# Chunk 7's routing logits from VectorE's dot products instead of TensorE's matmuls, in a three-stage kernel

## The chip, the cores and the metric

The kernel runs on one core of a Trainium2 chip. The metric is the device time of one execution in microseconds. Before the change three runs gave 766.73, 768.21 and 768.28 us; the median is 768.21. The profiled execution took 771.43 us.

## What is computed

The reference has three stages, one behind the other, all in float32:

```python
scores = q @ k^T / sqrt(64)           # 4 batches, 8 heads, 576 positions
scores = where(0 <= i-j < 128, scores - slope[h]*|i-j|, -1e9)
x = softmax(scores) @ v               # -> 2304 tokens x 512
h = x @ w_in                          # 512 -> 2048
x = (h * clip(h + 3, 0, 6) / 6) @ w_out
xn = x / (|x| + 1e-6); en = expert_emb / (|expert_emb| + 1e-6)
logits = xn @ en.T / tau              # 8 experts
e = argmax(logits); gate = softmax(logits)[e]
out = gate * (relu(x @ w1[e]) @ w2[e])   # each token by its one expert
```

## The kernel before, in words

The 2304 tokens are nine chunks of 256. Attention of the later chunks runs in the gaps of the dense layer of the earlier ones; for chunks 7 and 8 of the dense layer there is no attention left. A chunk's dense layer is eight up groups (`gemm1`, L720: 24 matmuls into `h_ps`) and eight down groups (`gemm2`, L773: 12 matmuls that add up in two banks `y_ps`); every float32 product is three passes over operands split in a high and a low part. Between an up group and its down group lie ScalarE's `u` (L730), VectorE's gate on `u` (L740), ScalarE's high part `gh` (L744) and VectorE's low part `gl` (L750). TensorE's stream alternates: up group i+2, down group i, up group i+3, down group i+1.

When a chunk's last down group is done, a `Route` object decides which expert takes each of its tokens. `rows` scales the two banks by 1/6 into `ys` and stores them to `ybuf`; `norms` sums their squares. The 8 logits of each token come in one of two ways:

- Chunks 0 to 6: `spread` loads half of the normalised expert embeddings, the same 4 x 512 numbers in every partition (`en_all`, a tile of 8 KB per partition, 1 MB in all), and `dots` lets VectorE multiply and sum, one instruction of 512 elements for each expert and half chunk (L834, and a short one that reads the sum).
- Chunks 7 and 8: `flip` transposes `ys` on TensorE and copies it back (`yT`), `logits` multiplies it with the embeddings (`lgT`), `total` adds four partial rows (`lg`).

`choose` takes the largest logit, its expert as a row of zeros and a one (`oh`) and the running count of tokens (`seen`). `ranks` (L880, L881) and `place` give each token its slot in its expert's list, which POOL scatters to `slots` in DRAM (L896). Behind chunk 7's `place`, `rank_experts(False)` sorts the experts by their counts so far (`ps_n`, L924). With that, SP reads the two largest experts' numbers, loads their weights (`st`, L1023, L1026) and the first lists (`ids`, L984), POOL gathers the rows (`xg`, L1001), and ScalarE and VectorE split the weights (`w_e`, L161, L162), all during chunk 8's dense layer. Chunk 8's tokens are routed while the first expert runs.

What sets the order: each piece of work is entered at a step by `at(step, ...)`, and the steps are played in order. One step unit is 1/1.91 of an up and a down group. TensorE carries out its instructions in exactly that order. On the other engines a scheduler orders the instructions by its own estimates. `ends(c)` is the step of chunk c's last down group; the numbers in `ROUTE` and `DOTS` are added to it.

The tiles for weights are one pool of 17 (`wp`, tag "w"); 16 hold the dense layer's split weights, and from chunk 1 on the one left takes the halves of `en_all`, one after the other. A weight tile is free when its last matmul of chunk 8 has read it.

Of the kernel before, what the change touches and what calls it, by code (L numbers as in the profile page):

```python
# [9 lines left out]
F32 = mybir.dt.float32  # L10
# [51 lines left out]
P_BUFS, V_BUFS = 2, 2  # L62
FLIPS_AHEAD = 0.01

ROUTE = (1, 1.43, 2.92, 4.5)
DOTS = ((-3.5, 4.5), (0.8, 1.0), (7.4, 0.8), 10.9, 12.28)
PLACE_C = 4.3

TOTAL = 0.95
PLACE_0 = (6.5, 10.6, 6.7, 2.08, 2.2, 1.0, 8.6)  # L70
# [27 lines left out]
def tile_kernel(  # L98
# [13 lines left out]
    nc = tc.nc  # L112
    B, H, S, D = q.shape
    NT, DM = out.shape
    DFF = w_in.shape[1] // 2
    NE = w1.shape[0]
# [3 lines left out]
    NCH = NT // CH  # L120
# [13 lines left out]
    wp = main.enter_context(tc.tile_pool(name="wp", bufs=17))  # L134
# [10 lines left out]
    def two_k(name, shape=(128, 512), dt=F32):  # L145
        return keep.tile(list(shape), dt, tag="f", bufs=5, name=name)

    def small(name, shape, dt=F32, bufs=2):
        return keep.tile(list(shape), dt, tag=name, bufs=bufs, name=name)
# [25 lines left out]
    for p in range(NP):  # L175
# [12 lines left out]
        out=whole, in_=whole, compare_op=ALU.is_ge, fill=MASKED, base=128, pattern=[[-1, 256]], channel_multiplier=1  # L188
    )
    nc.gpsimd.affine_select(  # L190
        out=whole, in_=whole, compare_op=ALU.is_ge, fill=MASKED, base=-1, pattern=[[1, 256]], channel_multiplier=-1
# [3 lines left out]
    for kinds in ((2, 2), (2, 0), (2, 1), (1, 2), (0, 2)):  # L195
        tables[kinds] = t = const.tile([128, 192], BF16, name="table%d%d" % kinds)
        for h, kind in enumerate(kinds):
            r = slice(64 * h, 64 * h + 64)
# [19 lines left out]
    half, share = fixed[:, 0:2], fixed[:, 2:3]  # L218
# [7 lines left out]
        out=earlier, in_=earlier, compare_op=ALU.is_gt, fill=0.0, base=0, pattern=[[1, 128]], channel_multiplier=-1  # L226
# [5 lines left out]
        out=fold, in_=ident.rearrange("p (g e) -> p e g", g=KD)[:, 0:NE, :], axis=AX.X, op=ALU.add  # L232
# [549 lines left out]
    class Route:  # L782
        def __init__(self, c):
            self.c = c

        def copy(self, t):
            c = self.c
# [25 lines left out]

        def norms(self):
            self.ss = small("ss", (128, 2))
            if self.c < NCH - 2:
                self.junk = two_k("junk")
            for t in range(2):
                ys = self.ys[t]
                to = self.junk if self.c < NCH - 2 else ys  # L820
                nc.scalar.activation(out=to, in_=ys, func=AF.Square, accum_out=self.ss[:, t:t + 1])
            self.rn = rn = small("rn", (128, 2))
            nc.gpsimd.tensor_tensor(out=rn, in0=self.ss, in1=half, op=ALU.pow)

        def spread(self, half):
            self.en = wp.tile([128, NE // 2, DM], F32, tag="w", name="en_all")
            src = en_rows[NE // 2 * half:NE // 2 * (half + 1), :].rearrange("(o e) d -> o (e d)", o=1)
            nc.sync.dma_start(out=self.en.rearrange("p e d -> p (e d)"), in_=src.to_broadcast([128, NE // 2 * DM]))

        def dots(self, e):  # L830
            if e == 0:
                self.lg = small("lg", (128, 2, NE))
            for t in range(2):
                V.tensor_tensor_reduce(  # L834
                    out=self.junk, in0=self.ys[t], in1=self.en[:, e % (NE // 2), :],
                    scale=1.0, scalar=0.0, op0=ALU.mult, op1=ALU.add, accum_out=self.lg[:, t, e:e + 1],
                )

# [319 lines left out]
    def at(step, fn, *args):  # L1158
        todo[step].append((fn, args))
# [8 lines left out]
    def ends(c, i=NF2 - 1):  # L1168
        return 0.0 if c == 0 else begins(2) if c == 1 else begins(c, i) + FIRST[2]
# [240 lines left out]
        at(begins(BLANK[0] + n // 3, BLANK[1]), blank, n, n + 3)  # L1410
    for c in range(NCH - 1):
        g = ends(c)
        if c < NCH - 2:
            loads, *halves, d2, d3 = DOTS
            if c == 0:
                g, r = FIRST[0], route_0
            else:
                r = Route(c)
                at(g, r.rows)
                at(g + 0.3, r.norms)  # L1420
                for x in range(2):
                    at(g + (loads[x] if c > 1 or x else 0.6), r.spread, x)
                for e in range(NE):
                    x, y = divmod(e, NE // 2)
                    at(g + halves[x][0] + halves[x][1] * y, r.dots, e)
            at(g + d2 * (c > 0), r.choose)
            at(g + d3 * (c > 0) + PLACE_C * (c == 0), r.ranks)
            at(g + d3 * (c > 0) + PLACE_C * (c == 0), r.place)
            continue
        r = Route(c)  # L1430
        at(g, r.rows)
        d = ROUTE
        assert 0 < d[0] <= d[1] <= d[2] < d[2] + TOTAL < d[3]
        at(g + d[0], r.flip, 0)
        at(g + d[1], r.flip, 1)
        at(g + d[1], r.norms)
        at(g + d[2], r.logits)
        at(g + d[2] + TOTAL, r.total)
        at(g + d[2] + TOTAL, r.choose)
        at(g + d[3], r.ranks)  # L1440
        at(g + d[3], r.place)
    g = begins(NCH - 1)

    def close_attention():
# [1 line left out]
        pools["x"] = main.enter_context(tc.tile_pool(name="x2", bufs=1, side="right"))  # L1446

    at(g - 1, close_attention)
    assert g + PLACE_0[0] > ends(NCH - 2) + ROUTE[3]
    at(g + PLACE_0[0], rank_experts, False)  # L1450
    at(g + PLACE_0[0], load_order, False, 0)
    at(g + PLACE_0[6], load_ids, 0, range(n_first))
# [9 lines left out]
    g = ends(NCH - 1)  # L1462
# [8 lines left out]
    r = Route(NCH - 1)  # L1471
# [34 lines left out]
    for j in range(1, NE):  # L1506
# [6 lines left out]
        if j == 1:  # L1513
            s = PLACE_1
            loads = [s[0] + s[1] * i for i in range(4)]
            splits = [s[2] + s[3] * i for i in range(8)]
            ids, gets, turns = LATE[0] + 0.05, [s[4] + s[5] * t for t in range(n)], [s[8] + s[9] * t for t in range(n)]
        else:
            s = [x + b - 16 for x in NEXT]
            s[5], s[7], s[9] = NEXT[5], NEXT[7], NEXT[9]  # L1520
            loads = [s[0], s[1], s[2], s[3]]
# [155 lines left out]
```

## Time and profile before

| what | value |
|---|---|
| runs, median | 766.73, 768.21, 768.28 us; 768.21 |
| profiled execution | 771.43 us, span 769.70 |
| TensorE busy | 748.1 us, 97% of the span |
| VectorE, ScalarE, POOL busy | 523.2, 383.7, 186.8 us |
| mean granted clock | 0.993 |
| chunk 7's last down group to chunk 8's third | 474.76 to 494.34 us |

The span runs from the first to the last instruction of the execution; 1.73 us lie around it. An engine's timeline lists its instructions in order of time, equal ones together; in brackets stands how long the engine was idle before and what ended that. A busy time is from an instruction's start to its end, and on VectorE and ScalarE the next instruction starts up to 0.1 us before that end. The granted clock is a share of 2.4 GHz: 0.50 is 1.2 GHz.

### The profile page before, as it was taken

Reading aid. Unit: us, or ns where it says so; the run is one execution under the profiler, and the core shown is the slowest. Engines: PE = TensorE matmul, PEld = TensorE weight load, DVE = VectorE, ACT = ScalarE, POOL = GpSimd, SP = SyncE. Lnnn points to the kernel's source line nnn. Section 1 sums busy time; section 2 is a strip of 40 time slices with the busy share of each in tenths; the row PEclk is TensorE's granted clock in tenths of the full one; section 3 lists DMA queues with packets and bytes.
Section 4 is the critical chain, followed back from the end, with each engine's and each line's share of the span. In section 5 each row is a group of like instructions: output and inputs, shape, how many; then the busy total and the mean of one; then the engine's idle time right before and its main releaser. Section 6 shows DMA issues by size and latency. Waiting matters only on the chain.

```text
span 769.7 us, 16001 instructions
## 1 busy us (share of the span) xinstructions
PE 748.1 (97%) x5740; PEld 660.4 (86%) x5740; DVE 523.2 (68%) x1528; ACT 383.7 (50%) x896; POOL 186.8 (24%) x349
## 2 busy tenths in 40 slices
PE   7999999999999999999999999999899999999995
PEld 5666688898888888888888889878899999999994
DVE  4899989897679578687787672456546735635620
ACT  6858665553454534544535543357244543543510
POOL 3000013332232241512412331120322213313111
PEclk9999999999999999999999999999999999999998
DMA  9986432446656443343343300096278436647100
GB/s 223 335 280 189 139 65 45 104 121 86 102 135 175 67 140 93 68 131 94 89 125 93 134 12 28 2 288 207 64 255 260 163 130 215 207 139 262 42 27 28
DMA packets 159111, 103.20 MB, mean 134 GB/s; under 512 B 119420, under 2 KB 135932, under 8 KB 157233
## 3 DMA queue, kind: packets, MB, share of 16 engines
q1 hardware_dynamic: 155280, 92.53, 43.7%
q0 software_dynamic: 3744, 9.58, 3.7%
q8 instruction: 47, 0.77, 0.4%
q14 instruction: 40, 0.32, 0.1%
HBM read 87.71 MB, written 14.47 MB: 133 GB/s over the span
## 4 chain that ended last, share of the span: by engine, by line
PE 57%; issue 17%; DMA 14%; DVE 5%; POOL 3%; SPq 2%; ACT 1%; POOLq 0%; ACTq 0%; DVEq 0%
PE h_ps L720 19%; PE y_ps L773 18%; DMA out_dram<-ob,ids 5%; PE h_ps L707 4%; PE y_ps L764 4%; PE acc L675 3%; PE sc_ps L610 2%; DMA ids<-slots 2%; DVE junk L834 2%; DMA slots<-pays,dest 2%; PE ps_u L1043 2%; PE ps_pt L649 1%; DMA xg<-ybuf,ids 1%; DMA en_all<-en_rows 1%; DMA wst<-in_moe_w_in_dram 1%
## 5 line engine op out<-in xcount | busy, mean ns | idle before, releaser
L720 PEld LDWEIGHTS h_ps<-xs,w_i 128*128 128x128 f32 x1536 | 192.4, 191 | 6.1 <-issue 1.0
L720 PE MATMUL h_ps<-xs,w_i 128*128 128x256 f32 x1536 | 195.2, 283 | 0.0
L773 PE MATMUL y_ps<-w_o,gh 128*128 128x512 f32 x512 | 163.5, 401 | 1.0 <-ACT gh L744 1.0
L664 POOL TENSOR_SCALAR_AFFINE_SELECT ph<-ph 64x128 f32<-64x128 f32 x224 | 90.6, 405 | 182.1 <-ACT ph L656 134.2
L773 PEld LDWEIGHTS y_ps<-w_o,gh 128*128 128x128 f32 x512 | 91.6, 188 | 25.3 <-issue 6.0
L1043 PE MATMUL ps_u<-x,w_e 128*128 128x280 f32 (+5 forms) x768 | 105.4, 294 | 0.0
L162 DVE TENSOR_TENSOR w_e<-st,w_e 128x1024 fp32r<-128x1024 f32 x64 | 76.5, 1218 | 39.6 <-ACT w_e L161 39.5
L773 PE MATMUL y_ps<-w_o,gl 128*128 128x512 f32 x256 | 100.2, 391 | 1.4 <-DVE gl L750 1.4
L1043 PEld LDWEIGHTS ps_u<-x,w_e 128*128 128x128 f32 x768 | 100.5, 189 | 0.2
L834 DVE CUSTOM_DVE_ANT_0 junk<-ys,en_all 128x512 f32<-128x512 f32 x112 | 77.1, 688 | 21.2 <-DMA en_all<-en_rows 12.9
L1067 PE MATMUL ps_o<-hs,w_e 128*128 128x280 f32 (+4 forms) x576 | 79.7, 298 | 0.0
L1067 PEld LDWEIGHTS ps_o<-hs,w_e 128*128 128x128 f32 x576 | 77.9, 191 | 0.0
L730 ACT ACTIVATE u<-h_ps,three 128x512 f32<-128x512 f32 x72 | 49.0, 680 | 56.6 <-PE h_ps L720 32.5
L161 ACT CAST w_e<-st 128x1024 fp32r<-128x1024 f32 x64 | 65.6, 1049 | 18.7 <-DMA st<-in_moe_w_dram 7.8
L744 ACT CAST gh<-u 128x512 fp32r<-128x512 f32 x64 | 39.7, 620 | 65.0 <-DVE u L740 64.9
L740 DVE SCALAR_TENSOR_TENSOR u<-u,h_ps 128x512 f32<-128x512 f32 x72 | 49.1, 683 | 26.3 <-ACT u L730 25.4
L750 DVE TENSOR_TENSOR gl<-u,gh 128x512 fp32r<-128x512 f32 x64 | 46.0, 719 | 24.7 <-ACT gh L744 24.6
L633 ACT ACTIVATE pt<-pt,nm 128x128 f32<-128x128 f32 x112 | 44.2, 395 | 33.5 <-DVE pt L626 33.3
L773 PEld LDWEIGHTS y_ps<-w_o,gl 128*128 128x128 f32 x256 | 48.1, 188 | 13.5 <-DVE gl L750 2.7
L1142 POOL DMA_INDIRECT out_dram<-ob,ids x23 | 30.3, 1316 | 114.0 <-DVE ob L1141 102.9
L1051 ACT ACTIVATE hs<-ps_u 128x280 fp32r<-128x280 f32 (+5 forms) x64 | 25.6, 403 | 45.4 <-PE ps_u L1043 44.8
L1052 DVE SCALAR_TENSOR_TENSOR hs<-ps_u,hs 128x280 fp32r<-128x280 f32 (+5 forms) x64 | 27.9, 442 | 20.9 <-ACT hs L1051 20.6
(185 smaller groups left out, 990.9 us busy)
## 6 DMA issues: line engine op xcount, KB each, us to landing
st<-in_moe_w_dram SPq DMA_DIRECT2D x32, 512.0 KB, 5.0
st<-in_moe_w_dram SPq DMA_DIRECT2D x16, 1024.0 KB, 6.9
en_all<-en_rows SPq DMA_DIRECT2D x14, 1024.0 KB, 5.3
wst<-in_moe_w_in_dram SPq DMA_DIRECT2D x8, 1024.0 KB, 8.4
wst<-in_moe_w_out_dram SPq DMA_DIRECT2D x8, 1024.0 KB, 12.3
ybuf<-ys SPq DMA_DIRECT2D x18, 256.0 KB, 2.1
out_dram<-empty SPq DMA_DIRECT2D x18, 256.0 KB, 2.2
kr<-in_k_dram SPq DMA_DIRECT2D x48, 48.0 KB, 2.3
```

Source lines behind the costliest of these rows:

```text
L161: nc.scalar.copy(hi, src)
L162: eng.tensor_tensor(out=lo, in0=src, in1=words(hi), op=ALU.subtract)
L633: nc.scalar.activation(out=x, in_=x, func=AF.Exp, scale=-1.0, bias=nm[:, j:j + 1], accum_out=sums[h][:, j:j + 1])
L664: nc.gpsimd.affine_select(out=out, in_=x, compare_op=ALU.is_gt if out is prev else ALU.is_ge, fill=0.0, base=0, pattern=[[0, 2], [-1 if ou ...
L720: nc.tensor.matmul(hp[:, f, :], lhsT=w[:, a, kk, f * 128:(f + 1) * 128], rhs=xs[:, b, kk, :], start=(n == 0), stop=(n == 3 * KD - 1),)
L730: nc.scalar.activation(out=u, in_=hp, func=AF.Relu, bias=three, scale=1.0)
L740: V.scalar_tensor_tensor(out=u, in0=u, scalar=6.0, in1=h_t[c, i], op0=ALU.min, op1=ALU.mult)
L750: V.tensor_tensor(out=gl, in0=g, in1=words(gh), op=ALU.subtract)
L773: nc.tensor.matmul(y_t[c][t], lhsT=g[a][:, f, t * 128:(t + 1) * 128], rhs=w[:, b, f, :], start=(i == 0 and f == 0 and n == 0), stop=(i == ...
L834: V.tensor_tensor_reduce(out=self.junk, in0=self.ys[t], in1=self.en[:, e % (NE // 2), :], scale=1.0, scalar=0.0, op0=ALU.mult, op1=ALU.add ...
L1043: nc.tensor.matmul(ps, lhsT=w[:, a, kk, (f % 2) * 128:(f % 2) * 128 + 128], rhs=x[:, b, kk, c0:c1], start=(n == 0), stop=(n == 3 * KD - 1),)
L1067: nc.tensor.matmul(ps, lhsT=ws_t[j, 4 + f // 2][:, a, f % 2, d * 128:(d + 1) * 128], rhs=hs[:, b, f, 0:width(j)], start=(n == 0), stop=(n ...
```

## The change

Chunk 7 takes its logits from `spread` and `dots` too; only chunk 8 keeps `flip`, `logits` and `total`. Its steps are in `DOTS_7`. As the two halves of the embeddings are now wanted close behind each other, `spread` keeps them in two tiles: the first goes where chunk 6's second half was, the second into the tile of the weights that chunk 8's first up group was the last to read. `norms` writes its squares to `junk`, which the dots write as well.

```diff
-ROUTE = (1, 1.43, 2.92, 4.5)
+DOTS_7 = ((-3.0, 0.9), (0.5, 0.5), (2.5, 0.5), 4.5, 4.8)
...
+            self.en = {}
...
-            if self.c < NCH - 2:
+            if self.c < NCH - 1:
                 self.junk = two_k("junk")
...
-            self.en = wp.tile([128, NE // 2, DM], F32, tag="w", name="en_all")
+            self.en[half] = wp.tile([128, NE // 2, DM], F32, tag="w", name="en_all")
...
-                    out=self.junk, in0=self.ys[t], in1=self.en[:, e % (NE // 2), :],
+                    out=self.junk, in0=self.ys[t], in1=self.en[e // (NE // 2)][:, e % (NE // 2), :],
...
-        if c < NCH - 2:
-            loads, *halves, d2, d3 = DOTS
+        if c < NCH - 1:
+            loads, *halves, d2, d3 = DOTS if c < NCH - 2 else DOTS_7
...
-        r = Route(c)
-        at(g, r.rows)
-        at(g + d[0], r.flip, 0)
-        at(g + d[1], r.flip, 1)
-        at(g + d[1], r.norms)
-        at(g + d[2], r.logits)
-        at(g + d[2] + TOTAL, r.total)
-        at(g + d[2] + TOTAL, r.choose)
-        at(g + d[3], r.ranks)
-        at(g + d[3], r.place)
```

In the changed file the lines from `Route` on stand one lower (L835 for L834, L881 for L880).

On TensorE, at the end of chunk 8's second down group, its fourth up group and the ranking stood thus before (`rk` and `ps_n` are the ranking matmuls, `lg` the sum of chunk 7's logits):

```order
L773 MATMUL y_ps<-w_o,gl 128x512
L854 MATMUL lg<-fold,lgT 128x8 x2
L720 MATMUL h_ps<-xs,w_i 128x256 x24
L880 LDWEIGHTS earlier
L880 MATMUL rk<-oh,earlier 128x16
L881 LDWEIGHTS ones
L881 MATMUL rk<-seen,ones 128x16
L924 LDWEIGHTS ones
L924 MATMUL ps_n<-seen,ones 128x8
L773 MATMUL y_ps<-w_o,gh 128x512 x2
```

and now:

```order
L773 MATMUL y_ps<-w_o,gl 128x512
L720 MATMUL h_ps<-xs,w_i 128x256 x24
L881 LDWEIGHTS earlier
L881 MATMUL rk<-oh,earlier 128x16
L882 LDWEIGHTS ones
L882 MATMUL rk<-seen,ones 128x16
L925 LDWEIGHTS ones
L925 MATMUL ps_n<-seen,ones 128x8
L773 MATMUL y_ps<-w_o,gh 128x512 x2
```

The matmuls of `lg` are gone, as are further up those of `lgT` and the transposes `ps_y`; the ranking stands where it stood, between the fourth up group and the third down group.

On VectorE, up to `seen`, which the second ranking matmul reads, stood the gate and split of chunk 8's third up group and then the choice:

```order
L740 SCALAR_TENSOR_TENSOR u<-u,h_ps 128x512
L750 TENSOR_TENSOR gl<-u,gh 128x512
L865 TENSOR_REDUCE mx<-lg 128x2
L867 TENSOR_TENSOR pick<-lg,mx 128x16
L868 TENSOR_TENSOR sh<-lg,mx 128x16
L869 TENSOR_TENSOR pick<-pick,order 128x16
L875 TENSOR_TENSOR sh<-sh,rn 128x16
L870 TENSOR_REDUCE mx<-pick 128x2
L871 TENSOR_TENSOR oh<-pick,mx 128x16
L888 TENSOR_REDUCE den<-sh 128x2
L872 TENSOR_TENSOR seen<-seen,oh 128x8
```

Now the last dot products (each with the reading of its sum) are followed by the gate `u` of the fourth up group and then the choice, with the split `gl` of the fourth group between `oh` and `seen`:

```order
L835 ISA junk,lg<-ys,en_all 128x512
L835 ISA lg 128x1
L740 SCALAR_TENSOR_TENSOR u<-u,h_ps 128x512
L866 TENSOR_REDUCE mx<-lg 128x2
L868 TENSOR_TENSOR pick<-lg,mx 128x16
L869 TENSOR_TENSOR sh<-lg,mx 128x16
L870 TENSOR_TENSOR pick<-pick,order 128x16
L876 TENSOR_TENSOR sh<-sh,rn 128x16
L871 TENSOR_REDUCE mx<-pick 128x2
L872 TENSOR_TENSOR oh<-pick,mx 128x16
L750 TENSOR_TENSOR gl<-u,gh 128x512
L873 TENSOR_TENSOR seen<-seen,oh 128x8
```

The fourth group's gate and split, which stood behind the ranking, now stand ahead of `seen`.

On ScalarE, the casts `w_e` of the first expert's weights stood among `u` and `gh` of chunk 8's last four groups thus:

```order
L730 ACTIVATE u<-h_ps,three 128x512
L744 CAST gh<-u 128x512
L161 CAST w_e<-st 128x1024 x2
L730 ACTIVATE u<-h_ps,three 128x512
L161 CAST w_e<-st 128x1024
L744 CAST gh<-u 128x512
L161 CAST w_e<-st 128x1024 x2
L730 ACTIVATE u<-h_ps,three 128x512
L161 CAST w_e<-st 128x1024
L744 CAST gh<-u 128x512
L161 CAST w_e<-st 128x1024
L730 ACTIVATE u<-h_ps,three 128x512
```

and now:

```order
L730 ACTIVATE u<-h_ps,three 128x512
L744 CAST gh<-u 128x512
L161 CAST w_e<-st 128x1024 x3
L730 ACTIVATE u<-h_ps,three 128x512
L161 CAST w_e<-st 128x1024
L744 CAST gh<-u 128x512
L161 CAST w_e<-st 128x1024 x2
L730 ACTIVATE u<-h_ps,three 128x512
L744 CAST gh<-u 128x512
L161 CAST w_e<-st 128x1024 x2
L730 ACTIVATE u<-h_ps,three 128x512
L744 CAST gh<-u 128x512
```

Three casts instead of two stand ahead of the sixth group's `u`, and the seventh and eighth groups' are no longer interleaved with casts; VectorE's subtractions for the same weights follow the same pattern. On SP, the two spreads of chunk 7 now stand behind the last load of `v` and ahead of chunk 7's two stores to `ybuf`.

## Rows read from the trace of the kernel before

**Rows 1.** Page, section 1: engine, busy us, share of the span, instructions

```profile
PE 748.1 (97%) x5740; PEld 660.4 (86%) x5740; DVE 523.2 (68%) x1528; ACT 383.7 (50%) x896; POOL 186.8 (24%) x349
```

**Rows 2.** TensorE's timeline: start us, us, engine, line, operation, out<-in, shape, count

```profile
477.51 3.04 PE L720 MATMUL h_ps<-xs,w_i 128*128 128x256 f32 x24
480.38 1.04 PE L807 MATMUL ps_y<-ident,ys 128*128 128x128 f32 x8
...
493.74 0.18 PE L880 MATMUL rk<-oh,earlier 128*128 128x16 bf16 x1
...
494.34 0.71 PE L773 MATMUL y_ps<-w_o,gh 128*128 128x512 f32 x2
```

**Rows 3.** Chain of waits, an undisturbed pair of groups: start us, us, what

```profile
447.04 2.87 PE h_ps L720 x24
449.91 2.75 PE y_ps L773 x12
```

**Rows 4.** VectorE's timeline in chunk 6's dot products

```profile
425.74 0.69 DVE L750 TENSOR_TENSOR gl<-u,gh 128x512 fp32r<-128x512 f32 x1 [1.06 <-ACT gh L744]
...
430.69 0.08 DVE L834 DVE_READ_ACCUMULATOR2_ANT lg<- 128x1 f32 x1
...
431.29 0.68 DVE L834 CUSTOM_DVE_ANT_0 junk<-ys,en_all 128x512 f32<-128x512 f32 x1
...
432.01 0.69 DVE L834 CUSTOM_DVE_ANT_0 junk<-ys,en_all 128x512 f32<-128x512 f32 x1
```

**Rows 5.** VectorE's timeline around chunk 7's choice

```profile
477.49 0.69 DVE L750 TENSOR_TENSOR gl<-u,gh 128x512 fp32r<-128x512 f32 x1 [1.06 <-ACT gh L744]
...
490.96 0.17 DVE L865 TENSOR_REDUCE mx<-lg 128x2 f32<-128x16 f32 x1 [1.09 <-PE lg L854]
...
491.79 0.17 DVE L871 TENSOR_TENSOR oh<-pick,mx 128x16 bf16<-128x16 f32 x1
...
494.41 0.17 DVE L893 CAST dest<-den 128x2 int32<-128x2 f32 x1
```

**Rows 6.** Stretches around 554: us, busy by engine (instructions), granted clock, DMA share, GB/s

```profile
551.50:554.00 2.50, 0.08 (x1) 0.00 (x0) 0.00 (x0) 0.39 (x1) 1.89 (x3) 1.00 0.45 125
...
555.00:556.00 1.00, 1.00 (x6) 1.00 (x6) 0.23 (x1) 0.58 (x1) 0.29 (x1) 0.50 0.94 94
...
557.50:558.00 0.50, 0.50 (x5) 0.50 (x5) 0.00 (x0) 0.00 (x0) 0.00 (x0) 1.00 1.01 358
```

**Rows 7.** Chain of waits behind chunk 7's ranking

```profile
496.21 6.76 DMA slots<-pays,dest
```

**Rows 8.** SP's timeline: its transfers

```profile
503.09 1.49 SPq L984 DMA_DIRECT2D ids<-slots  x3
504.84 0.98 SPq L1023 DMA_DIRECT2D st<-in_moe_w_dram  x2
```

**Rows 9.** ScalarE's timeline, in brackets idle before and what ended it

```profile
510.39 1.05 ACT L161 CAST w_e<-st 128x1024 fp32r<-128x1024 f32 x1 [0.70 <-DMA st<-in_moe_w_dram]
```

**Rows 10.** Page, section 5: VectorE's subtraction for expert weights (mean ns of one)

```profile
L162 DVE TENSOR_TENSOR w_e<-st,w_e 128x1024 fp32r<-128x1024 f32 x64 | 76.5, 1218 | 39.6 <-ACT w_e L161 39.5
```

**Rows 11.** TensorE's timeline at chunk 8's sixth down group

```profile
512.04 0.73 PE L773 MATMUL y_ps<-w_o,gh 128*128 128x512 f32 x2 [0.61 <-ACT gh L744]
513.42 0.51 PE L773 MATMUL y_ps<-w_o,gl 128*128 128x512 f32 x1 [0.64 <-DVE gl L750]
```

**Rows 12.** TensorE's timeline, the first matmuls of the first expert

```profile
527.65 3.33 PE L1043 MATMUL ps_u<-x,w_e 128*128 128x280 f32 x24
```

**Rows 13.** VectorE's timeline, chunk 8's dest

```profile
538.88 0.16 DVE L893 CAST dest<-den 128x2 int32<-128x2 f32 x1
```

**Rows 14.** Stretches, the one between the transposes and the third down group

```profile
480.38:494.34 13.96, 13.61 (x106) 12.13 (x104) 4.86 (x20) 5.56 (x13) 0.72 (x1) 1.00 0.00 1
```

**Rows 15.** The tile en_all: its transfers from issue to landing

```profile
DMA to landing us min/median/max: 4.3/5.3/8.2
```

**Rows 16.** DMA issues, the scatters: count, median us from issue to landing

```profile
slots<-pays,dest POOLq DMA_INDIRECT x18, 5.4
```

More of the change, by code (lines that the diff above doesn't have):

```diff
@@ L819, in norms @@
                 ys = self.ys[t]
-                to = self.junk if self.c < NCH - 2 else ys
+                to = self.junk if self.c < NCH - 1 else ys
                 nc.scalar.activation(out=to, in_=ys, func=AF.Square, accum_out=self.ss[:, t:t + 1])
@@ L825, in spread @@
         def spread(self, half):
-            self.en = wp.tile([128, NE // 2, DM], F32, tag="w", name="en_all")
+            self.en[half] = wp.tile([128, NE // 2, DM], F32, tag="w", name="en_all")
             src = en_rows[NE // 2 * half:NE // 2 * (half + 1), :].rearrange("(o e) d -> o (e d)", o=1)
-            nc.sync.dma_start(out=self.en.rearrange("p e d -> p (e d)"), in_=src.to_broadcast([128, NE // 2 * DM]))
+            nc.sync.dma_start(out=self.en[half].rearrange("p e d -> p (e d)"), in_=src.to_broadcast([128, NE // 2 * DM]))
         def dots(self, e):
@@ L1429, in tile_kernel @@
             continue
-        r = Route(c)
-        at(g, r.rows)
-        d = ROUTE
-        assert 0 < d[0] <= d[1] <= d[2] < d[2] + TOTAL < d[3]
-        at(g + d[0], r.flip, 0)
-        at(g + d[1], r.flip, 1)
-        at(g + d[1], r.norms)
-        at(g + d[2], r.logits)
-        at(g + d[2] + TOTAL, r.total)
-        at(g + d[2] + TOTAL, r.choose)
-        at(g + d[3], r.ranks)
-        at(g + d[3], r.place)
     g = begins(NCH - 1)
@@ L1448, in tile_kernel @@
     at(g - 1, close_attention)
-    assert g + PLACE_0[0] > ends(NCH - 2) + ROUTE[3]
+    assert g + PLACE_0[0] > ends(NCH - 2) + DOTS_7[4]
     at(g + PLACE_0[0], rank_experts, False)
```

## Prediction

> **What bounds the kernel now.** I read the page's busy times first: TensorE is busy for 97% of the span [rows 1], so a change is worth what it does to TensorE's own stream, at the place where it stands. That place comes from TensorE's timeline over the end of chunk 7 and the start of chunk 8 [rows 2]. I call the 24 matmuls of one 256-wide piece of the first product an up group and the 12 of the second a down group. Between 477.5 and 494.3 us the stream runs without a gap: up and down groups of chunk 8, and between them the transposes of chunk 7's rows, the two sets of logit matmuls, and then the three little ranking matmuls. So what stands there is paid in full, and what is taken away is gained in full, as long as nothing new makes TensorE wait. Then I read VectorE's timeline one chunk earlier and at the same place, because the ranking matmuls need `oh` and `seen` from VectorE, and TensorE's order puts them ahead of chunk 8's third down group.
>
> **TensorE: what is removed.** From the second up group of chunk 8 to the first ranking matmul the trace has 493.74 - 477.51 = 16.23 us [rows 2]. What remains there after the change is three up groups of 2.87 and two down groups of 2.75 us [rows 3]: 14.11. The change takes 2.12 us out, and TensorE comes to the ranking matmul at 491.6 instead of 493.7.
>
> **VectorE: when the ranking's input is there.** The new order of the sixteen dot products up to the fifth is the one chunk 6 has now (a dot, the norm's two small instructions, dots, a gate `u`, dots). There the fifth dot starts 432.01 - 425.74 = 6.27 us after the split `gl` [rows 4]; that split is at 477.49 for chunk 7 [rows 5], so the fifth dot starts at 483.76. From it, a dot followed by a dot takes 432.01 - 431.29 = 0.72 us, and one followed by a gate or split 0.62 (an estimate: the row's 0.69 busy less the overlap of the next start); a gate or split takes 431.29 - 430.69 = 0.60 [rows 4]. Of the twelve dots left, eight are followed by a dot and four by a gate or split: 8 x 0.72 + 4 x 0.62 = 8.24. Four gates or splits stand among them and behind them, the last being the `u` of chunk 8's fourth up group, which now stands ahead of the choice: 2.40. So `mx` starts at 494.40. From `mx` to `oh` is 491.79 - 490.96 = 0.83 [rows 5], and `oh` ends some 0.13 later. Then comes the split of the same fourth group, 0.60, and only then `seen`, 0.15: TensorE has what the second ranking matmul needs at about 496.1. It has stood since 491.6: an idle stretch of 4.5 us. From the ranking matmul to the next down group was 494.34 - 493.74 = 0.60 [rows 2], so that group starts at 496.75 instead of 494.34: **+2.4 us**, the gain of 2.12 included. Every instruction behind the ranking on TensorE waits with it. The scatter of the slots, which POOL issues once `dest` is there (494.41, [rows 5]), moves by the same 2.4.
>
> **TensorE's clock.** The trace has one long pause in the second half. TensorE is busy for 0.08 of the 2.5 us before 554.0, after that the granted clock is 0.50 (the level of 1.2 GHz) and it is back at 1.00 from 557.5 [rows 6]. Half of those 3.4 to 3.5 us is lost, 1.7. The pause here is nearly twice as long and I expect the same fall: TensorE is 2.4 + 1.7 = 4.1 late after it. The Trainium skill (TensorE: Matmul & The Clock Gate, section What's actually happening) says that how many matmuls run slowly varies from run to run of one kernel. By that this term lies between 0 and 1.7 in a given execution and TensorE between 2.4 and 4.1 late; the only clean pause of this half of the trace shows the fall. This raises the chance of the smaller loss below and leaves the sum alone, because of the next part.
>
> **The loads behind the ranking.** SP waits for the scatter (6.76 us from its issue to its end, [rows 7]) before it loads the ids at 503.09, and the second pair of expert weights at 504.84 is queued behind them [rows 8]. So that pair moves by 2.4 too. ScalarE casts it at 510.39, when it has landed [rows 9]: now 512.8. Here the order has changed: the third cast and its subtraction on VectorE now stand ahead of the `u` of chunk 8's sixth up group. Cast 1.05 to 513.85 [rows 9], subtraction 1.2 [rows 10] to 515.05, gate 0.60 to 515.65, the fourth subtraction 1.2 to 516.85, split 0.60 to 517.45. The sixth down group's third matmul, which waits for that split, stood at 513.42 [rows 11]: **+4.0 us**. TensorE on its own leg would be there at 513.42 - 0.61 - 0.64 + 4.1 = 516.3, or 514.6 without the clock's fall, so the loads end last in both cases and I take +4.0. The two down groups behind it I leave as they are: the order there loses one wait (an `u` no longer interleaved) and adds one (both last casts ahead of the last `u`), which I can't price better than -0.7 to +1.
>
> **Chunk 8's own choice.** It keeps the old form, but its surroundings are ordered anew: one more weight subtraction stands ahead of `dest` on VectorE, and one cast ahead of the copy of `lgT` on ScalarE. `dest` came 538.88 - 527.65 = 11.23 us after the first matmul of the first expert [rows 12, 13], and what follows it (scatter, ids, gather) ends the pause before 554.0. The price lies between 0 (it fits an idle stretch) and 1.2 [rows 10]; I take 0.9.
>
> **What I cost at nothing.** The two spreads are 2 MB. In 480.4 to 494.3 the DMA share is 0.00 [rows 14], so they disturb no one. The second waits for the first up group of chunk 8, done when chunk 7's last down group begins, 477.51 - 2.75 = 474.76 [rows 2, 3], and lands 4.3 to 8.2 us after its issue [rows 15], by 483.0 at the latest; its first reader is the ninth dot, at 483.76 + 3 x 0.72 + 0.62 + 0.60 = 487.1. If that cover of 4.1 us went, each us beyond it would delay the ranking by one. On ScalarE the two copies of `yT` and one of `lgT` go; it isn't waited for there. PSUM banks become free, and nothing waits for one.
>
> **Sum.** 4.0 + 0.9 = 4.9 us. The profiled execution is 771.43 us (span 769.70 and 1.73 around it), 3.2 above the median of the timed runs; it would be 776.3. Added to the median of 768.21: **773.1 us**.
>
> **Rivals.** (1) The dots hide as those of chunks 1 to 6 do, and TensorE keeps its 2.12 us: 766.1. For it speaks that VectorE is far from full [rows 1] and that DMA is quiet. Against it: chunks 1 to 6 have their ranking several groups later, and here sixteen dots of 0.72, some 11.5 us, with gates and splits among them and the choice behind, stand between chunk 7's last rows and 491.6. VectorE would have to be 4.5 us earlier. (2) The stall stays but the loads are less late: the scatter takes 5.4, the median of all 18 [rows 16], or the clock stays up. Then the loads' leg is +2.6 and TensorE's +1.2 to +2.9, and with 0.6 for chunk 8 the time is 771.4. (3) The dots end at 491 to 494 and the pause is half as long without a fall of the clock: no change, 768 to 769. (4) The order at the end of chunk 8 costs its upper bounds (+1, and 1.2 instead of 0.9), or the pause before 554.0 grows: +6.2 to +7.5, about 775.
>
> **Chances.** Forecast (3.8 to 6 us slower) 0.50; (2) 0.24; (4) 0.13; (3) 0.06; (1) 0.07. The three slower cases make 0.87 for slower by over 0.2%, about 1.5 us, which is what a measurement of this kernel can tell from no change. The range leaves out (1), (3) and the far ends of (2) and (4): 769.5 to 776.0.
>
> **What would show it.** Right: a pause on TensorE before the ranking matmul of 4 to 5 us that ends with `seen`; granted clock near 0.5 for some 3 us behind it; the third cast of the expert's weights about 2.4 us later than now and standing ahead of `u`; a wait of the sixth down group for `gh` and `gl`. Wrong: no pause there (the dots were faster or stand elsewhere), a pause but the loads land as early as now, or a wait of the ninth dot for its spread.

## The result, and the profile after

The changed kernel took 773.74 us in the median of 11 runs (771.57 to 776.12), the kernel before, run again beside it, 768.21 (766.73 to 773.12, 11 runs). The ratio over all runs is 1.0057 with a 95% interval of 1.0042 to 1.0072, so 4.4 us slower (3.2 to 5.5); the medians by themselves are 5.5 apart, the means (773.51 and 769.03) 4.5. 773.1 had been forecast. Of the four runs of dots4 in the table below, one took 4148.15 us, and the median there is that of the other three. The profiled execution took 774.05 us, span 772.3, against 771.43 and 769.70 before. The profiles are thus only 2.6 us apart; why is part of what follows.

Everything of the profile after lies 1.64 us later from the start of chunk 8's second up group on: it begins at 479.15 instead of 477.51 [rows 2]. What runs before it on TensorE is the same in both; the shift arises at the start of the program (the matmul behind a wait of 1.46 us for ScalarE's `ph` stands at 24.49 before and at 26.52 after). It is not the change's: in the twelve other profiles of this study the group begins between 474.09 and 476.31, without and with the dots. Times below are therefore counted from that group in each profile. "The stretch" is the time from there to the first matmul of the first expert: 50.14 us before [rows 2, 12], 53.38 after.

TensorE's timeline after (start us, us, engine, line, operation, out<-in, shape, count, in brackets idle before and what ended it; the row at 532.53 counts up to 535, where its view ends):

```profile
479.15 3.04 PE L720 MATMUL h_ps<-xs,w_i 128*128 128x256 f32 x24
...
490.39 3.03 PE L720 MATMUL h_ps<-xs,w_i 128*128 128x256 f32 x24
497.19 0.20 PE L881 MATMUL rk<-oh,earlier 128*128 128x16 bf16 x1 [3.77 <-DVE oh L872]
497.86 0.17 PE L882 MATMUL rk<-seen,ones 128*128 128x16 bf16 x1 [0.47 <-DVE seen L873]
498.43 0.17 PE L925 MATMUL ps_n<-seen,ones 128*128 128x8 bf16 x1 [0.40 <-DVE seen L895]
498.45 1.20 PE L773 MATMUL y_ps<-w_o,gh 128*128 128x512 f32 x2
...
503.15 3.05 PE L720 MATMUL h_ps<-xs,w_i 128*128 128x256 f32 x24
...
518.23 0.73 PE L773 MATMUL y_ps<-w_o,gh 128*128 128x512 f32 x2 [0.81 <-ACT gh L744]
519.31 0.50 PE L773 MATMUL y_ps<-w_o,gl 128*128 128x512 f32 x1 [0.35 <-DVE gl L750]
...
532.53 2.69 PE L1044 MATMUL ps_u<-x,w_e 128*128 128x280 f32 x19
...
559.36 0.66 PE L1014 MATMUL ps_x<-ident,xg 128*128 128x128 f32 x4 [1.81 <-DMA xg<-ybuf,ids]
```

This answers to [rows 2, 11, 12]. The fourth up group ends at 493.42, and then comes what the forecast rested on: 3.77 us idle until `oh`, 0.47 until `seen`, 0.40 until the next `seen`, 4.64 in all. VectorE's timeline at the same place says why:

```profile
481.34 0.69 DVE L835 CUSTOM_DVE_ANT_0 junk<-ys,en_all 128x512 f32<-128x512 f32 x1 [1.52 <-ACT junk L822]
...
485.40 0.69 DVE L835 CUSTOM_DVE_ANT_0 junk<-ys,en_all 128x512 f32<-128x512 f32 x1
...
488.82 0.69 DVE L835 CUSTOM_DVE_ANT_0 junk<-ys,en_all 128x512 f32<-128x512 f32 x1
...
495.53 0.68 DVE L740 SCALAR_TENSOR_TENSOR u<-u,h_ps 128x512 f32<-128x512 f32 x1
496.13 0.16 DVE L866 TENSOR_REDUCE mx<-lg 128x2 f32<-128x16 f32 x1
...
496.95 0.17 DVE L872 TENSOR_TENSOR oh<-pick,mx 128x16 bf16<-128x16 f32 x1
497.04 0.69 DVE L750 TENSOR_TENSOR gl<-u,gh 128x512 fp32r<-128x512 f32 x1
497.65 0.15 DVE L873 TENSOR_TENSOR seen<-seen,oh 128x8 bf16<-128x8 bf16 x1
...
498.55 0.17 DVE L894 CAST dest<-den 128x2 int32<-128x2 f32 x1
```

Answering to [rows 4, 5]: the sixteen dots run from 481.34 to 495.5 with gates and splits among them; the `u` of the fourth group stands ahead of `mx`, its `gl` between `oh` and `seen`. The first dot waited 1.52 us for ScalarE's norms, which write the tile `junk` that the dots write too. The ninth dot, at 488.82, waits for nothing: the second spread was there. The stretches behind the pause (us, busy us by engine with instructions in the order PE, PEld, DVE, ACT, POOL; granted clock, DMA share, GB/s):

```profile
500.00:502.00 2.00, 2.00 (x6) 1.52 (x5) 0.92 (x10) 0.00 (x0) 1.00 (x2) 0.50 0.02 1
502.40:503.15 0.75, 0.75 (x5) 0.59 (x3) 0.00 (x0) 0.00 (x0) 0.00 (x0) 0.95 0.00 0
503.15:506.00 2.85, 2.85 (x25) 2.85 (x24) 0.00 (x0) 0.00 (x0) 0.00 (x0) 1.00 0.75 18
560.50:562.00 1.50, 1.50 (x14) 1.50 (x13) 0.69 (x1) 0.14 (x1) 0.19 (x1) 1.00 0.58 79
```

Answering to [rows 6]: the granted clock is 0.50 behind the pause, and the third down group, 498.45 to 503.15, takes 4.70 us instead of 2.75 [rows 3]. Later, behind the pause of 1.81 us ahead of the late rows (those that come last to the first expert), the clock stays at 1.00; before, it had fallen there behind this pause:

```profile
554.03 1.09 PE L1013 MATMUL ps_x<-ident,xg 128*128 128x128 f32 x4 [2.45 <-DMA xg<-ybuf,ids]
```

SP's timeline after, with the ids and the second pair of weights, and then ScalarE's, with the first three casts and the sixth group's `gh`, answering to [rows 8, 9]:

```profile
507.83 1.49 SPq L985 DMA_DIRECT2D ids<-slots  x3
509.58 0.98 SPq L1024 DMA_DIRECT2D st<-in_moe_w_dram  x2
```

```profile
510.87 1.05 ACT L161 CAST w_e<-st 128x1024 fp32r<-128x1024 f32 x1 [2.58 <-DMA st<-in_moe_w_dram]
512.37 1.05 ACT L161 CAST w_e<-st 128x1024 fp32r<-128x1024 f32 x1 [0.45 <-DMA ids<-slots]
514.61 1.05 ACT L161 CAST w_e<-st 128x1024 fp32r<-128x1024 f32 x1 [1.20 <-DMA st<-in_moe_w_dram]
...
517.55 0.62 ACT L744 CAST gh<-u 128x512 fp32r<-128x512 f32 x1 [0.36 <-DVE u L740]
```

The second pair of weights is issued 30.4 us into the stretch (27.3 before), the third cast begins at 35.5 (32.9 before), and `gh` of the sixth group stands behind it.

### The profile page after: what moved, and what is told of

The parts are those of the page before. It is cut to its first block, busy times and chain, and to the rows that moved or that the text cites. A ratio compares the mean times of both kernels' runs of the same rounds, so it can differ in the third digit from the quotient of the medians.

```text
span 772.3 us, 15980 instructions
## 1 busy us (share of the span) xinstructions
PE 746.2 (97%) x5712; PEld 658.1 (85%) x5712; DVE 533.1 (69%) x1560; ACT 381.5 (49%) x893; POOL 187.4 (24%) x349
## 5 line engine op out<-in xcount | busy, mean ns | idle before, releaser
L835 DVE CUSTOM_DVE_ANT_0 junk<-ys,en_all 128x512 f32<-128x512 f32 x128 | 88.4, 690 | 21.5 <-DMA en_all<-en_rows 11.4
```

Source lines behind the costliest of these rows:

```text
L835: V.tensor_tensor_reduce(out=self.junk, in0=self.ys[t], in1=self.en[e // (NE // 2)][:, e % (NE // 2), :], scale=1.0, scalar=0.0, op0=ALU.m ...
```

## The experiments

Each row of the table is one profiled execution and its timed runs; ratio and interval are against the kernel before on the same chip. Its median was 768.21 us for the first two rows and 764.2 to 765.0 for the others, so rows are compared by their ratios and not by their medians. "Idle at rk" is TensorE's idle time before the first ranking matmul. "To late rows" is from chunk 8's second up group to the first matmul `ps_u<-w_e,x`, on the rows that come last to the first expert; it holds what the change touches. Behind it the profiled times of all fourteen kernels have 210.2 to 211.3 us left.

| kernel | median us | ratio (95%) | idle at rk | stretch | to late rows |
|---|---|---|---|---|---|
| before | 768.21 | | 0 | 50.14 | 82.58 |
| the change | 773.74 | 1.0057 (1.0042 to 1.0072) | 3.77 | 53.38 | 84.60 |
| dots4 | 772.26 | 1.0104 (1.0077 to 1.0131) | 7.19 | 57.02 | 87.42 |
| ownsq | 768.21 | 1.0045 (1.0031 to 1.0059) | 2.46 | 51.88 | 83.05 |
| fill | 769.48 | 1.0063 (1.0038 to 1.0088) | 0.20 | 53.09 | 84.22 |
| ids | 770.05 | 1.0079 (1.0058 to 1.0100) | 3.77 | 52.64 | 83.75 |
| fillids | 769.00 | 1.0071 (1.0047 to 1.0094) | 0.20 | 53.70 | 84.28 |
| late1 | 765.15 | 1.0009 (0.9999 to 1.0020) | 1.02 | 50.41 | 80.30 |
| casts | 769.75 | 1.0080 (1.0059 to 1.0101) | 3.77 | 52.10 | 84.68 |
| all4 | 767.85 | 1.0046 (1.0029 to 1.0062) | 0 | 46.06 | 82.65 |
| bcasts | 768.77 | 1.0055 (1.0039 to 1.0072) | 0 | 47.11 | 83.71 |
| rows8 | 766.91 | 1.0035 (1.0022 to 1.0049) | 0 | 46.28 | 81.08 |
| brows8 | 768.02 | 1.0049 (1.0032 to 1.0065) | 0 | 47.10 | 82.63 |
| rows8b | 764.52 | 1.0000 (0.9985 to 1.0016) | 0 | 47.68 | 78.06 |

### Do VectorE's dots set the pause? (dots4, ownsq)

dots4 computes experts 6 and 7 twice:

```diff
-            for t in range(2):
+            for t in range(2) if (self.c, e // 2) != (NCH - 2, 3) else (0, 1, 0, 1):
```

> The changed kernel with four more dot products: experts 6 and 7 of chunk 7 are computed twice, so nothing but VectorE's time grows. The stretch from chunk 8's second up group to the first expert's first matmul is 53.4 us in the changed kernel and 50.1 in the one before. Theory (VectorE's dots decide when the ranking has its input, and everything behind it waits): 4 x 0.72 = 2.9 us more pause ahead of the ranking (3.8 becomes 6.6), scatter, ids and second pair of weights 2.9 later, stretch 56.3, time about 2.9 us above the changed kernel's (776 to 777). Rival (the time is lost elsewhere, by the two 1 MB spreads or by the order on ScalarE): pause longer, but stretch and time within 0.7 us of the changed kernel's (773 to 774).

TensorE's timeline at the ranking in dots4, with the idle time in brackets:

```profile
495.82 0.20 PE L881 MATMUL rk<-oh,earlier 128*128 128x16 bf16 x1 [7.19 <-DVE oh L872]
...
496.51 0.17 PE L925 MATMUL ps_n<-seen,ones 128*128 128x8 bf16 x1 [0.33 <-DVE seen L895]
```

In all 7.52 us idle instead of 4.64: 2.88 more, which is 4 x 0.72. The stretch grew by 3.6, since the sixth down group waits 1.71 us instead of 1.16 as well; the casts ahead of it stand in another order. The time is 7.9 us above before on its chip, against 4.4 for the change: 3.5 more, where 2.9 had been expected. That the time is lost elsewhere falls.

ownsq gives the norms a tile of their own:

```diff
-                to = self.junk if self.c < NCH - 1 else ys
+                to = self.junk if self.c < NCH - 2 else two_k("sq") if self.c < NCH - 1 else ys
```

> The changed kernel with one edit: chunk 7's norms write their squares to a tile of their own and not to junk, which the dots write as well, so that VectorE's first dot need not wait for ScalarE (1.52 us in the changed kernel's profile). VectorE's order also moves: the split gl of the fourth group comes behind seen. Theory (the pause's length is set by the start of the dots and what stands among them): oh 1.5 and seen 2.1 us earlier, pause 2.2 instead of 3.8, ids and second pair of weights 2.1 earlier, stretch about 51.3 instead of 53.4, time 2 us below the changed kernel's. Rival (the dots wait for something else that is there no earlier, as the first spread): pause and stretch as before.

The ranking comes 1.3 us earlier (1.5 had been expected) and the stretch is 1.5 shorter (2.1 expected); that `junk` is shared is a part of the loss. In the timed runs the two intervals overlap.

### Which leg ends last behind the ranking? (fill, ids, fillids, late1, casts)

A leg is here one of the two chains that meet at the sixth down group: TensorE's own stream, and the loads with their casts.

fill puts matmuls of the identity into the pause:

```diff
+            warm(16 * (self.c == NCH - 2))
             self.rk = rk = bank([128, 2, NE], "rk")
```

> The changed kernel with 16 matmuls of the identity by itself on TensorE, ahead of the ranking, that fill most of the pause of 3.8 us. Theory: the granted clock stays at 1.00 behind the pause, the third down group takes 2.8 us instead of 4.0 after the ranking and the stretch up to the sixth group comes about 1.9 us earlier, but the sixth down group then waits that much longer for its loads: its third matmul where it was, stretch 53.4 +- 0.4, time as the changed kernel (772 to 774). Rival (TensorE's own leg, pause and slow clock, sets the time): stretch 51.5, time 1.9 us less (770 to 772). If the clock falls all the same, the pause is not what lowers it.

The stretches behind the ranking in fill (columns as above, the granted clock third from the end):

```profile
493.90:495.00 1.10, 1.10 (x6) 0.93 (x6) 0.98 (x7) 0.00 (x0) 0.53 (x1) 1.00 0.07 15
495.00:496.00 1.00, 1.00 (x6) 0.83 (x5) 0.98 (x9) 0.00 (x0) 0.69 (x2) 1.00 0.00 0
```

TensorE's timeline of fill at the sixth down group:

```profile
512.63 0.73 PE L773 MATMUL y_ps<-w_o,gh 128*128 128x512 f32 x2 [1.61 <-ACT gh L744]
513.99 0.50 PE L773 MATMUL y_ps<-w_o,gl 128*128 128x512 f32 x1 [0.63 <-DVE gl L750]
```

With the pause filled the clock stays at 1.00, so it is the idle time that lowers it, and the fifth up group starts 22.2 us into the stretch instead of 24.0. But the sixth down group now waits 1.61 and 0.63 us instead of 0.81 and 0.35, and 0.3 us is left of the gain: the loads end last.

ids loads the first lists behind the second pair of weights:

```diff
-PLACE_0 = (6.5, 10.6, 6.7, 2.08, 2.2, 1.0, 8.6)
+PLACE_0 = (6.5, 10.6, 6.7, 2.08, 2.2, 1.0, 8.9)
```

> The changed kernel with the loads of the first lists (ids) behind the first expert's second pair of weights in SP's queue instead of ahead of it, so that this pair does not wait for the scatter. Theory (the loads end last at the sixth down group): the cast of the second pair is at least 2 us earlier, the waits of 0.8 and 0.35 us of the sixth down group go, and the stretch shrinks by 1.0 to 1.5 us to about 52; more is not to be had because TensorE's own leg stands only 1.2 us behind the loads. Rival (these waits come from the order on VectorE and ScalarE and not from the loads): waits and stretch as in the changed kernel, 53.4.

Gained 0.7 us instead of 1.0 to 1.5. The sixth group's waits are nearly gone (0.46 is left), but ScalarE's order moved: the first cast now stands ahead of the fifth group's `gh`, and that group waits 0.38. With both edits together:

> Both at once: the 16 filling matmuls and the ids behind the second pair of weights. Theory (two legs, the later one decides): TensorE's leg is 1.9 us earlier by the clock and the loads no longer hide it, so the stretch is 3.0 us shorter (50.4) and the time about 3 us less than the changed kernel's, about that of the kernel before. Rival (only one of the two legs ever counts): the gain is that of the better of the two alone.

ScalarE's timeline of fillids at the fifth group, and TensorE's:

```profile
499.34 0.69 ACT L730 ACTIVATE u<-h_ps,three 128x512 f32<-128x512 f32 x1 [7.34 <-PE h_ps L720]
505.33 1.04 ACT L161 CAST w_e<-st 128x1024 fp32r<-128x1024 f32 x1 [5.30 <-DMA st<-in_moe_w_dram]
506.28 0.61 ACT L744 CAST gh<-u 128x512 fp32r<-128x512 f32 x1
```

```profile
506.95 1.22 PE L773 MATMUL y_ps<-w_o,gh 128*128 128x512 f32 x2 [2.03 <-ACT gh L744]
```

The stretch of time behind this wait:

```profile
506.90:508.00 1.10, 1.05 (x2) 0.50 (x2) 1.10 (x2) 0.97 (x1) 0.00 (x0) 0.50 1.09 346
```

This expectation failed, as did its rival: 53.70, no gain at all. The two legs were not all. `gh` of the fifth group sits on ScalarE behind a cast that waits 5.30 us for the first pair of weights, which was never behind the ids; TensorE waits 2.03 us for it, and behind that wait the granted clock is 0.50 until 510.3, so the fall that the filling matmuls had removed comes back there. What holds TensorE is any cast in ScalarE's order whose transfer is not there, and every transfer for the first expert starts behind the ranking.

late1 moves the ranking behind the third down group:

```diff
-DOTS_7 = ((-3.0, 0.9), (0.5, 0.5), (2.5, 0.5), 4.5, 4.8)
+DOTS_7 = ((-3.0, 0.9), (0.5, 0.5), (2.5, 0.5), 4.5, 5.9)
-PLACE_0 = (6.5, 10.6, 6.7, 2.08, 2.2, 1.0, 8.6)
+PLACE_0 = (7.4, 10.6, 7.45, 1.83, 1.45, 1.0, 8.6)
```

> The changed kernel with chunk 7's ranking (rk, ps_n and what follows) one down group later in TensorE's order, behind the third down group of chunk 8 instead of ahead of it; the first weight load is entered later by as much. The third down group (2.75 us) then runs while VectorE still computes dots, so most of TensorE's pause and the slow clock behind it go, and the scatter and the loads come no earlier than in the changed kernel; two casts instead of three stand ahead of the sixth group's u. Theory (loads and the casts that stand among u and gh decide): the sixth down group waits 2 us or more for gh and gl, and the stretch from chunk 8's second up group to the first expert (53.4 in the changed kernel, 50.1 before) shrinks only by what the one cast less gives, 1 to 2.5 us, to 51 to 52.5. Rival (TensorE's pause and clock set the time): 2.75 for the filled pause and 1.9 for the clock come back in full, 48.8.

ScalarE's timeline of late1 at the sixth group, and TensorE's:

```profile
506.41 1.05 ACT L161 CAST w_e<-st 128x1024 fp32r<-128x1024 f32 x1 [6.72 <-DMA st<-in_moe_w_dram]
507.99 1.05 ACT L161 CAST w_e<-st 128x1024 fp32r<-128x1024 f32 x1 [0.53 <-DMA ids<-slots]
508.94 0.68 ACT L730 ACTIVATE u<-h_ps,three 128x512 f32<-128x512 f32 x1
510.94 0.62 ACT L744 CAST gh<-u 128x512 fp32r<-128x512 f32 x1 [1.31 <-DVE u L740]
```

```profile
511.61 0.73 PE L773 MATMUL y_ps<-w_o,gh 128*128 128x512 f32 x2 [2.78 <-ACT gh L744]
```

The clock behind this wait:

```profile
508.80:511.60 2.80, 0.03 (x1) 0.00 (x0) 1.96 (x5) 1.49 (x4) 1.34 (x2) 1.00 1.05 362
511.60:513.00 1.40, 1.39 (x5) 0.89 (x6) 1.14 (x2) 1.40 (x2) 1.09 (x2) 1.00 1.04 386
```

The stretch is 50.41, 0.6 below the theory's range and 1.6 above the rival's value. TensorE does wait for `gh` behind two casts, 2.78 us, as the theory has it, but that is shorter than the gain, and the granted clock stays at 1.00 behind it. This move takes back nearly the whole loss: no difference from the kernel before can be told. It does two things at once, as expected: it fills the pause and takes the third cast from ahead of `u`. The ranking itself comes no earlier (18.03 us into the stretch, 18.04 in the changed kernel).

casts enters the casts later and moves `rows` to POOL:

```diff
-PLACE_0 = (6.5, 10.6, 6.7, 2.08, 2.2, 1.0, 8.6)
+PLACE_0 = (6.5, 10.6, 6.7, 2.08, 6.30, 1.0, 8.6)
-            V.tensor_scalar(out=rows, in0=ids, scalar1=NT - CH, scalar2=None, op0=ALU.min)
+            nc.gpsimd.tensor_scalar(out=rows, in0=ids, scalar1=NT - CH, scalar2=None, op0=ALU.min)
```

> The changed kernel with the casts and subtractions of the first expert's weights entered 4.1 steps later, and the three little instructions that clamp the ids (rows) on POOL, which gathers with them, instead of on VectorE; the ranking and the pause stay. Theory (the loads' leg is these casts, subtractions and rows, which stand ahead of the fifth to seventh groups' u and gh and wait for transfers): no wait of the fifth and sixth down groups for gh or gl is left, the stretch shrinks by the 1.2 us that they waited, to 52.2, unless the four casts that now stand ahead of the seventh group's u make that one wait. Rival (the waits come from TensorE's pause itself, by groups that follow too closely): waits and stretch as in the changed kernel.

The stretch is 52.10, and there is no wait of the fifth to eighth groups: as expected. The time gained nothing, though: chunk 8's choice, among casts now, was 1.2 us slower (28.0 us from the first expert to the late rows, 26.8 in the changed kernel).

### Can the gain be had? (all4, bcasts, rows8, brows8, rows8b)

all4 has the edits of ownsq, late1 and casts together, with

```diff
-PLACE_0 = (6.5, 10.6, 6.7, 2.08, 2.2, 1.0, 8.6)
+PLACE_0 = (7.4, 10.6, 7.45, 1.83, 5.55, 1.0, 8.6)
```

> The changed kernel with everything that the pause and its sequel are put down to taken away together: norms write to a tile of their own (so the first dot needs not wait for them, 1.4 us), the ranking stands behind the third down group, rows are clamped on POOL, and casts are entered 4.1 steps later. Theory: TensorE hardly waits, at most 1 us at the ranking, the clock stays up, no wait of the fifth and sixth down groups; three up and two down groups less the old 2.12 us: stretch 46 to 47.5, against 53.4 in the changed kernel and 50.1 before; time 2.5 to 4 us below the kernel before of the same chip. Rival (the dots cost by themselves, by VectorE or DMA contention): stretch above 50, not faster than before.

TensorE's timeline of all4 at chunk 8's logits, then ScalarE's, then the stretches of that time:

```profile
524.79 0.65 PE L845 MATMUL lgT<-yT,enT 128*32 128x128 f32 x16
530.00 1.02 PE L855 MATMUL lg<-fold,lgT 128*128 128x8 f32 x4 [4.57 <-ACT lgT L850]
```

```profile
523.66 1.04 ACT L161 CAST w_e<-st 128x1024 fp32r<-128x1024 f32 x1
528.04 0.63 ACT L822 ACTIVATE ys<-ys 128x512 f32<-128x512 f32 x1 [3.34 <-DMA ybuf<-ys]
...
529.59 0.36 ACT L850 COPY lgT<-lgT 128x256 f32<-128x256 f32 x1
```

```profile
525.40:530.00 4.60, 0.04 (x4) 0.00 (x0) 0.56 (x1) 1.96 (x7) 0.52 (x1) 0.74 0.82 313
530.00:532.00 2.00, 2.00 (x9) 2.00 (x10) 1.59 (x10) 1.99 (x3) 0.21 (x1) 0.50 0.02 8
```

The stretch is 46.06, as expected: 4.1 us less than before. But the time is 1.0046 of before. ScalarE's norms of chunk 8, which overwrite `ys`, wait 3.34 us for the store of these rows, TensorE 4.57 for the logits behind them, and the clock falls. That store stands behind the weights of two experts, with the DMA engines at 1.04 to 1.07 from 505 to 525.

bcasts edits the kernel before:

```diff
-PLACE_0 = (6.5, 10.6, 6.7, 2.08, 2.2, 1.0, 8.6)
+PLACE_0 = (6.5, 10.6, 6.7, 2.08, 5.30, 1.0, 8.6)
-            V.tensor_scalar(out=rows, in0=ids, scalar1=NT - CH, scalar2=None, op0=ALU.min)
+            nc.gpsimd.tensor_scalar(out=rows, in0=ids, scalar1=NT - CH, scalar2=None, op0=ALU.min)
```

> The kernel before, with rows on POOL and the casts entered 3.1 steps later, nothing else. Theory: the waits of its sixth and seventh down groups (0.61 + 0.64 + 0.36 + 0.35 us) go: stretch 48.2 to 49 instead of 50.1, time 1 to 2 us below before. This is what the load order gives without the dots; what all4 has beyond it is the dots' own part, about 2 us. Rival: no change, 50.1, when those waits have another cause.

The stretch is 47.11, one us better than expected, and the gain is lost again at the same place (32.1 us from first expert to late rows). So 3.0 of the 4.1 us that all4 gains in the stretch come without the dots, from the order of the casts and from `rows` on POOL. The other 1.05 are put down to the dots, though all4 also enters the casts a step later. rows8 and brows8 are all4 and bcasts (casts 3.1 steps later in both) with one more rule, that the second expert's loads wait for the store (only the condition of the edit is shown):

```diff
+                if j == 1:
+                    tc.add_manual_dep(x.ins, stored[-1].ins.name, PLACED, reason="chunk 8's rows first")
```

> As all4 (own tile for the norms, ranking behind the third down group, rows on POOL, casts 3.1 steps later), and the loads of the second expert's weights wait for chunk 8's rows to be stored. In all4 the stretch was 46.1 us as expected, but chunk 8's choice lost it again: 3.3 us in which ScalarE's norms waited for the store of ybuf, queued behind 8 MB of weights with the DMA engines at 0.99, then 4.6 us idle on TensorE and the slow clock. Theory (that is the whole loss): stretch 46 again, from the first expert's first matmul to its late rows (31.6 in all4, 26.4 before) 24 to 26, time 4 to 7 us below the kernel before of the same chip, faster than both kernels. Rival (the transfers are the bound whatever their order, 8 MB after the ranking): the second expert then waits for its weights and the time is within 2 us of before.

> The kernel before with the same edits of what comes behind the ranking (rows on POOL, casts 3.1 steps later, second expert's weights behind chunk 8's rows), without the dots. Theory: stretch 47 (as in bcasts, 47.1), first expert to late rows 24 to 26 instead of bcasts' 32.1, time 3.5 to 6 us below before. The difference to rows8 is what chunk 7's dots are worth when nothing waits for them: the 2.1 us of TensorE, less the 1 us or so that it waits at the ranking; so 1 us in favour of rows8. Rival: no difference between the two, or brows8 ahead, if the later ranking costs rows8 its 2 us in the loads.

TensorE's timeline of rows8 in the first expert's second product:

```profile
538.45 1.03 PE L1072 MATMUL ps_o<-hs,w_e 128*128 128x280 f32 x6 [1.18 <-DVE hs L1057]
...
542.57 8.61 PE L1072 MATMUL ps_o<-hs,w_e 128*128 128x280 f32 x50 [3.08 <-DVE rounds L966]
```

The choice is undisturbed in both (0.49 us idle at the logits), but the first expert's second product then waits 1.18 and 3.08 us (1.17 and 3.08 in brows8) for the last casts and VectorE's subtractions, which now come behind it, and the clock falls once more. The times miss their expectations by 6.6 us and more. In rows8 4.3 of it are these waits and some 2 the clock (0.50 to 0.58 until 547). The rest is put down to the ruler, which no run tests: the expectations were reckoned from the profiled execution of before, 3.2 us above its median (below). Between the two, rows8 is 0.8 us shorter in the stretch and 1.1 us in the median (intervals overlap). rows8b sets the casts closer:

```diff
-PLACE_0 = (7.4, 10.6, 7.45, 1.83, 4.55, 1.0, 8.6)
+PLACE_0 = (7.4, 10.6, 7.45, 1.83, 5.15, 0.6, 8.6)
```

> As rows8, with the eight casts of the first expert's weights 0.6 steps apart from each other instead of 1, so that all eight stand ahead of chunk 8's last gh. In rows8 the stretch was 46.3 us and chunk 8's choice undisturbed, but the last three casts and subtractions came behind it and the second product of the first expert waited 1.18 and 3.08 us for them. Theory (that is all that is left): these 4.3 us go, the late rows are there in time (16.75 us behind rk in late1, so at about 545, TensorE comes at 546.8), the time from chunk 8's second up group to the second product's end shrinks from 81.1 to about 77 (82.6 in the kernel before), time 762 to 763.5 against 764.3 of before. Rival (the weights that land behind the ranking are the bound): the two casts more ahead of the eighth group wait for transfers, the stretch grows by 1 to 3 us, and the time is within 1.5 us of before or above it.

TensorE's timeline of rows8b, its two longest waits:

```profile
517.57 0.73 PE L773 MATMUL y_ps<-w_o,gh 128*128 128x512 f32 x2 [1.29 <-ACT gh L744]
...
540.42 4.78 PE L1072 MATMUL ps_o<-hs,w_e 128*128 128x280 f32 x35 [0.92 <-DVE hs L1057]
```

It falls between theory and rival: 78.06 to the late rows instead of 77, and the stretch 1.4 us longer than in rows8, as the rival has it, with the eighth group waiting 1.29 us for `gh` behind two casts and the second product 0.92. The time is that of the kernel before (764.52 against 764.96), as the rival has it too. No kernel of the study beats the one before clearly.

## Why the prediction was right, step by step

**TensorE and VectorE.** TensorE came to the ranking 14.3 us into the stretch (forecast 14.1), the fifth dot started at 6.25 (forecast 6.25), `mx` at 16.98 (16.89), `seen` ended at 18.65 (18.6), the pause was 4.64 (4.5), and the third down group started 2.47 us later than before (2.4). Chunk 6's timeline, which has the same order of dots, gates and splits, was the right ruler. The stream before was not quite without a gap: TensorE is busy for 13.61 of the 13.96 us [rows 14], and the other 0.35 is a wait of `ps_n` ahead of the third down group. It lies in the 0.60 that the forecast kept, so no sum changes.

**The clock.** It fell, and cost 1.95 us (forecast 1.7). That it didn't matter in the sum was also right: fill removes it and gains 0.3. The changed kernel's eleven runs had mean granted clocks of 0.990 to 0.993. The Trainium skill (TensorE: Matmul & The Clock Gate, section What's actually happening) says, of a kernel's first matmuls, that the count of slow ones varies from run to run of one kernel. The traces agree at the start of the program, where both kernels are alike: behind the same wait of 1.46 us the granted clock was 0.50 from 25.0 to 28.4 before and stayed at 1.00 after.

**The loads.** The second pair was issued 3.1 us later (forecast 2.4: `dest` came 2.5 later, and the scatter landed in up to 7.4 us instead of 6.8) and cast 2.6 later, and the sixth down group's third matmul came 4.25 us later (forecast 4.0). The reason given, second pair of weights behind the ids, was a part of it: ids and fillids showed that the first pair binds as much, since it too is asked for only when the ranking is known. casts confirmed the order on ScalarE and VectorE as the link.

**The stretch as a sum on TensorE.** The waits that the timelines show add up to 2.31 us before (0.35 at `ps_n`, 0.61, 0.64, 0.36 and 0.35 at the sixth and seventh groups) and to 5.80 after (4.64 and 1.16). With 1.95 for the clock and 2.12 for the matmuls that are gone, the stretch should grow by 5.80 + 1.95 - 2.31 - 2.12 = 3.3 us; it grew by 3.24. In late1 the waits are 4.67 and the clock holds: 0.24 by the sum, 0.27 measured.

**What was mis-sized.** The seventh and eighth groups gave 1.0 us back (forecast 0, between -0.7 and +1, so outside these bounds): the waits of the seventh, 0.36 and 0.35 us before, are gone, and no wait of the eighth shows in their place. Chunk 8's `dest` came 0.59 later relative to the first expert and the late rows 0.45 (forecast 0.9). And the profile of before holds 1.67 us which the change did not touch but the profile after lacks: from the late rows' first transpose to `ps_u<-w_e,x` are 6.06 us before and 4.39 after, because the pause ahead was 2.45 us with a fall of the clock before, and 1.81 us without one after. Together: 1.64 (start) + 3.24 (stretch) + 0.45 - 1.67 - 1.04 (behind it) = 2.6, the difference of the spans.

**What was luck.** The change's own part in the two profiles is 3.24 + 0.45 = 3.7 us, where 4.9 was forecast; 4.4 (3.2 to 5.5) was measured over all runs. That 773.1 lies so close to the median of 773.74 is thus luck in part. The profile of before also was no usual one: besides the fall of the clock at the end of the program, which all fourteen profiles have, it holds one at 25.0 and one at 554.0, some 3.4 us at 0.50 each, which cost 1.7 us each by the forecast's reckoning, together about the 3.2 us by which it stood above its median. On the four other chips the 59 runs of the kernel before had mean granted clocks of 0.994 to 0.998, with a median of 0.997; the profile of before has 0.993, and the profiles with the fall at the end alone, fill and rows8b, have 0.996 and 0.997. So the usual execution of before has neither of the two falls on those chips. On the first chip, where no clocks of before's runs are on record, that is argued. From the table the usual value of before to the late rows would be 79 to 80 us and not 82.58: late1 has 80.3 there and a profiled run 1.6 us above before's median, fill 84.2 and 5.1, rows8b 78.1 and 2.2 below.

**Rivals.** (1), dots hidden, fell with the pause. (2) fell: the scatter took 7.4 us and not 5.4, the clock did not stay up, and the loads were as late as forecast; but what the profiles show of the change, 3.7 us, lies nearer to its 3.2 than to 4.9. (3), half the pause and no fall, fell with 4.64 us and 0.50. (4) was not reached. That the time could be won back by order alone (late1: the ranking one down group later) stood in no rival.

## What to carry to other kernels

Moving work to an engine with spare time pays only if its result is there when the busy engine's order asks for it: place the consumer (here the ranking) by when the new producer ends, not where it stood. Behind a decision that starts large loads, the engines that convert those loads hold whatever stands behind them in order; look at each cast ahead of a gate or split and ask when its transfer lands. A wait taken away in a chain of such engines mostly shows up at the next one: check the whole stretch, not the wait.

## What the runs showed of the hardware that was not expected

Pauses of TensorE of like length had different sequels: 2.03 us (fillids), 2.45 (before), 2.46 followed by 0.78 (ownsq), 3.77 (the changed kernel) and 4.57 (all4) brought the granted clock to 0.50, while 2.78 (late1) and 1.81 (the changed kernel, late rows) left it at 1.00. The loads behind the ranking keep the DMA engines at 1.02 to 1.08 of the profile's measure for 20 us (510 to 530 in the changed kernel, 320 to 380 GB/s), and in all4 the store of chunk 8's rows, 2 x 256 KB, which takes 2.2 us in the median, took from 519.7 to 528.0 among them.
